# Softmax attention beside linear attention on one core: first loads in use order, a level of sums on GpSimd, a last chain over more banks

## The chip, the cores and the metric

The program runs on one core of a Trainium2 chip. The metric is device time in microseconds. The kernel before took 773.87 us (median of 7 runs, 771.07 to 775.39). A separate profiled execution took 772.23 us; its recorded span is 770.5 us.

## The reference

Two attention layers run on their own inputs, and their outputs are set side by side. In both, S = 2048 tokens, D = 512, H = 32 heads of Dh = 16, and everything is bfloat16.

```python
# A: softmax attention
scores = einsum("bhqd,bhkd->bhqk", q, k) * Dh ** -0.5
o = einsum("bhqk,bhkd->bhqd", softmax(scores), v)
# B: linear attention with a learned feature map
pq, pk = q @ w_phi, k @ w_phi                       # per head, 16 x 16
phi = concatenate([softmax(p), softmax(-p)])        # 32 features, for q and for k
kv, z = einsum("bhsf,bhsd->bhfd", phi_k, v), phi_k.sum(s)
o = (phi_q @ kv) / (phi_q @ z + 1e-6)
# both: o @ wo; out[:, 0:512] is A, out[:, 512:1024] is B
```

## The kernel before

**A.** The work is cut into 32 units: 8 groups g of four heads by 4 chunks c of 512 queries. A unit has 16 key tiles (`kt`, 128 keys). Each key tile of a unit has four pieces, one a head: TensorE multiplies 32 rows of `KT` with 32 rows of `QT` into a bank of PSUM (`kq`, L748). From there a key tile goes one of two ways. On the ScalarE way (`act_kt`, `act_exp`, L962), one activation takes exp of two or three pieces at once. On the VectorE way (`dve_kt`), four `tensor_scalar` (L1020) write the bits of a float16 exponential as uint16, and three more (L1031) shift these by a quarter step each. TensorE then adds V times the exponentials into the unit's bank (L755): four matmuls a key tile for ScalarE, sixteen for VectorE. `src_a` and `src_d` deal the key tiles out as the engines come free, so more room on VectorE means fewer key tiles for ScalarE, and the other way round.

When a unit is complete, VectorE copies its bank to `X` (L803). The sums in it go by DMA to `sums`, VectorE takes reciprocals (L817), two more DMAs spread these to `Yd` (L820, L823), GpSimd multiplies (L835), and every eight units the output projection follows (L1076, L1091, L1094).

**B** runs in between. Its weights are folded with `w_phi` into `Wf`. Sixteen `k_step` make the keys' features for 128 tokens each: two exponentials on ScalarE (L1172), the sum of each 16 on VectorE (L1175), a reciprocal (L1178), two products on GpSimd (L1182), V's projection, and the product with V (L1202, L1211). Sixteen `q_step` do the queries.

**Head.** SP and ScalarE issue the first loads (L575 to L590). Four blocks of 128 rows of x are transposed on TensorE in two halves (L607), each of which ScalarE (L618) or VectorE (L621) copies out; then come the first Q and K projections (`proj`, `first_k`, L649, L693). The weight `va` says up to which key tile ScalarE copies every second V tile out, and `ka` how many of the eight copies of the first pair's K are ScalarE's (L677, L699). For the later K tiles, VectorE copies out (L659), GpSimd masks one copy (L685) and VectorE masks the other in place (L687, stream `dv_ek`).

**Tail.** The last unit doesn't use the DMAs: a matmul with `sel` spreads its sums (L852), VectorE (L862) and ScalarE (L866, L868) take reciprocals, VectorE multiplies (L870), then sixteen matmuls (L877) and four (L883) make the last 512 rows of A, copied out at L1088 and L1091 and stored at L1094. `range_check` (L900) counts sums that are out of range; its flag decides whether `_general`, another whole path, runs. The program ends with a wait for every DMA queue's semaphore.

**Order.** Nothing is decided on the chip. `_Sched` (L158) runs when the program is built: it holds a queue of tasks for each purpose (`SC.stream`), each with a weight, and always places the task with the least start time plus weight, by its own durations and latencies. The outcome is one fixed instruction order per engine, with semaphores between. `_W` holds the weights, and `_AT` changes them after every 16 key tiles. `port=True` marks VectorE work that the planner keeps from lying beside GpSimd's, and each GpSimd task waits for the last such VectorE task (L322). Fill matmuls (L782) keep TensorE at work.

Of the kernel before, what the change touches and what calls it, by code (L numbers as in the profile page):

```python
# [26 lines left out]
class _Stream:  # L27
    def __init__(self, key, sem, step):
        self.key = key
        self.sem = sem  # L30
        self.step = step
        self.seq = 0
        self.items = []
        self.known = {}

# [18 lines left out]
class _Plan:  # L54

    def __init__(self):
        self.streams = {}

# [15 lines left out]
    def dma(self, queue_key, dma_key, fn, deps=()):  # L74
# [3 lines left out]
        d.seq += 1  # L78
        clock = dict(q.known)
# [78 lines left out]
class _Sched:  # L158
# [147 lines left out]
    def _place(self, t, start):  # L306
# [41 lines left out]
        if t.then is not None:  # L348
# [5 lines left out]
          dek=-0.081, av=-0.051, kf=-0.03, v=0.039, kv=0.004, qf=-0.012, y=-0.203, t=0.061, o=0.243, df=-0.163,  # L354
          dred=-0.076, dv=-0.053, dkv=-0.118, dy=-0.02, dd=0.003, dob=-0.078, dmn=0.041, akf=-0.019,
          aqf=-0.089, aot=-0.317, age=0.03, early=0.0, guard=0.346, cut=5, lead=6, b0=0.286, b1=0.54, b2=0.99,
          p0=8, p1=30, p2=6.012, el=2, va=16, ka=8, dm=0.4, force=0.41, fill=0.575, dg=9.0)
_AT = (
    (16, dict(qd_r=0.028, pa_n=4, pd_w=-0.018, dx=-0.13, dev=-0.185, kf=0.191, t=0.016, dred=-0.015, dv=-0.112,
         dkv=-0.099, lead=5, el=3)),  # L360
    (32, dict(dev=-0.176, dad=0.08, av=-0.024, v=-0.015, dred=-0.03, dkv=-0.263, aot=-0.267, cut=6)),
    (48, dict(dx=-0.161, dn=-0.142, da=-0.093, dek=-0.193, o=0.174, dred=0.092, dkv=-0.169)),
    (64, dict(pa_w=0.186, da=-0.041, t=-0.143, dmn=0.088, aqf=-0.05, force=0.401)),
    (80, dict(qa=-0.09, b=-0.016, dek=-0.392, kf=0.176, o=0.066, dy=-0.045, dd=0.081, guard=0.393, force=0.423,
         fill=0.523)),
    (96, dict(qa=-0.035, qd_r=0.115, pa_n=3, pa_w=0.053, pd_w=0.071, b=-0.067, dx=-0.205, dev=-0.361, dn=-0.232,
         da=-0.165, dad=0.033, dek=-0.081, av=-0.051, kf=-0.03, v=-0.004, qf=0.039, t=0.061, o=0.243, dred=-0.076,
         dv=-0.053, dkv=-0.118, dy=-0.02, dd=0.003, dmn=0.089, aqf=-0.113, aot=-0.317, guard=0.346, cut=5, el=2,
         force=0.41, fill=0.575)),
    (112, dict(b=0.054, dv=-0.088, cut=6)),  # L370
    (128, dict(qa=-0.01, qd_o=0.258, pj=-0.023, pa_n=4, dev=-0.337, kf=-0.125, kv=0.138)),
    (144, dict(tp=-0.289, dad=0.017, dek=-0.071, t=0.114, dred=0.027, dy=-0.048, lead=6)),
    (160, dict(df=-0.044, dv=-0.151)),
    (176, dict(pa_n=5, b=-0.012, dev=-0.315, dop=-0.47, dn=-0.205, dek=0.033, t=0.113, df=0.024, dv=-0.086,
         guard=0.24)),
    (192, dict(op=-0.055, o=0.219, dv=-0.15, dd=-0.02)),
    (208, dict(kv=0.114, dv=-0.241, akf=-0.029, force=0.418, dg=1.5)),
    (224, dict(qa=-0.012, qd_r=0.032, pa_n=3, pa_w=-0.038, pd_w=0.067, dxe=-0.184, dop=-0.475, dad=-0.077,
         dek=0.117, av=0.012, v=-0.084, dkv=-0.112, dd=0.046, dob=0.031, aqf=-0.094)),
    (240, dict(b=-0.066, dx=-0.217, dop=-0.41, av=-0.009, v=-0.137, o=0.178, dred=0.076, guard=0.364, fill=0.583)),  # L380
    (256, dict(pd_n=1, op=-0.011, dek=0.165, t=0.142, o=0.381, aqf=-0.185)),
    (272, dict(qd_o=0.274, b=-0.197, dev=-0.216, av=-0.01, t=0.14, dv=-0.326, cut=5, lead=5, force=0.436)),
    (288, dict(pj=-0.091, kf=-0.045, dred=0.192, dy=-0.179, force=0.414)),
    (304, dict(qd_r=0.056, pa_n=2, op=0.004, dev=-0.175, dek=0.12, t=0.103, dd=0.078, el=3)),
    (320, dict(dn=-0.079)),
    (336, dict(qd_r=0.128, b=-0.244)),
# [21 lines left out]
def _main_path(nc, es, P, dsem, flag, A_x, A_wqkv, A_wo, B_x, B_wqkv, B_w_phi, B_wo, out):  # L408
# [440 lines left out]
    def last_unit(xv, xi, c):  # L849
# [6 lines left out]
        for k in range(4):  # L856
            cs = slice(128 * k, 128 * k + 128)
            bc = bcs[k // 2]
            def y_at(t, cs=cs):
                return Yd[:, parts[0][0].res["y"].idx if parts else t.res["y"].idx, cs]  # L860
# [1468 lines left out]
```

## Time and profile before

| what | us |
|---|---|
| median of 7 runs | 773.87 |
| profiled execution, its time | 772.23 |
| its span | 770.5 |
| ScalarE busy | 745.1 |
| TensorE busy | 730.1 |
| VectorE busy | 724.3 |
| GpSimd busy | 151.2 |
| first L962 starts | 10.65 |
| last X copy (L803) starts | 758.05 |

Busy time counts overlapping ends of neighbouring instructions, and TensorE's most of all, since matmuls are pipelined: VectorE's L1020 has a mean of 683 ns, but four in a row took 2.47 us. A line of the stretches view gives a stretch, its length, each engine's busy time with its number of instructions, TensorE's granted clock, and the DMA share and rate. A line of the groups gives the line, engine, operation and tiles, the count, the busy time and the mean, and the idle time before them with what ended it.

### The profile page before, as it was taken

Reading aid. Unit: us, or ns where it says so; the run is one execution under the profiler, and the core shown is the slowest. Engines: PE = TensorE matmul, PEld = TensorE weight load, DVE = VectorE, ACT = ScalarE, POOL = GpSimd, SP = SyncE. Lnnn points to the kernel's source line nnn. Section 1 sums busy time; section 2 is a strip of 40 time slices with the busy share of each in tenths; the row PEclk is TensorE's granted clock in tenths of the full one; section 3 lists DMA queues with packets and bytes.
Section 4 is the critical chain, followed back from the end, with each engine's and each line's share of the span. In section 5 each row is a group of like instructions: output and inputs, shape, how many; then the busy total and the mean of one; then the engine's idle time right before and its main releaser. Section 6 shows DMA issues by size and latency. Waiting matters only on the chain.

```text
span 770.5 us, 17249 instructions
## 1 busy us (share of the span) xinstructions
PE 730.1 (95%) x7209; PEld 217.4 (28%) x7209; DVE 724.3 (94%) x1315; ACT 745.1 (97%) x846; POOL 151.2 (20%) x218
## 2 busy tenths in 40 slices
PE   8999999999899999999999999999999999999996
PEld 3322222223222222223222223322222222222222
DVE  1799999999799999999999999999999999999996
ACT  6999999999799999999999999999999999999994
POOL 3321111110102131312122113232222113122120
PEclk9999999999899999999999999999999999999999
DMA  6200000017300110000000010000000001010002
GB/s 151 69 3 23 11 15 19 16 26 139 97 12 15 30 34 15 6 16 17 18 16 19 16 32 17 9 18 23 26 23 22 26 21 34 16 32 29 11 25 65
DMA packets 43871, 23.38 MB, mean 30 GB/s; under 512 B 31180, under 2 KB 39820, under 8 KB 43788
## 3 DMA queue, kind: packets, MB, share of 16 engines
q1 hardware_dynamic: 42204, 21.45, 10.3%
q8 instruction: 57, 0.93, 0.5%
q10 hardware_dynamic: 1584, 0.79, 0.5%
q14 instruction: 26, 0.21, 0.1%
HBM read 11.81 MB, written 4.45 MB: 21 GB/s over the span
## 4 chain that ended last, share of the span: by engine, by line
ACT 87%; PE 7%; DVE 3%; DMA 2%; issue 0%; SPq 0%; ACTq 0%
ACT pT L962 82%; PE PS L755 2%; PE PS L748 2%; ACT e_k L1172 2%; ACT eT L1235 1%; DMA sums<-X 1%; DVE rg L1020 1%; DMA OT<-in_A_x_dram 1%; DVE rg L1031 1%; ACT Wf L1235 1%; PE PS L877 0%; ACT KT L677 0%; ACT VP L657 0%; DVE Wf L1157 0%; PE PS L646 0%; DMA scr<-rin 0%
## 5 line engine op out<-in xcount | busy, mean ns | idle before, releaser
L962 ACT ACTIVATE pT<-PS 128x1024 bf16<-128x1024 f32 (+1 forms) x755 | 707.0, 1095 | 6.7 <-PE PS L748 6.6
L1020 DVE TENSOR_SCALAR rg<-PS 128x512 uint16<-128x512 f32 x524 | 340.1, 683 | 11.4 <-PE PS L748 9.6
L748 PE MATMUL PS<-QT,KT 32*128 32x512 bf16 x2048 | 318.0, 387 | 21.4 <-ACT pT L962 14.6
L1031 DVE TENSOR_SCALAR rg<-rg 128x2048 uint16<-128x2048 uint16 x393 | 256.5, 688 | 1.3 <-PE PS L755 0.9
L748 PEld LDWEIGHTS PS<-QT,KT 32*128 32x128 bf16 x2048 | 80.6, 91 | 286.5 <-ACT pT L962 226.8
L755 PE MATMUL PS<-pT,VP 128*32 128x512 bf16 x1524 | 151.0, 390 | 4.2 <-ACT pT L962 2.0
L755 PE MATMUL PS<-rg,VJ 128*32 128x512 f16 x1572 | 144.8, 388 | 3.8 <-DVE rg L1031 3.3
L755 PEld LDWEIGHTS PS<-pT,VP 128*32 128x32 bf16 x1524 | 39.1, 94 | 82.5 <-issue 51.3
L1182 POOL TENSOR_TENSOR w<-e_k,stat 128x512 bf16<-128x512 bf16 x32 | 33.1, 1056 | 119.7 <-DVE stat L1178 68.2
L755 PEld LDWEIGHTS PS<-rg,VJ 128*32 128x32 bf16 x1572 | 38.3, 95 | 54.2 <-issue 22.1
L755 PE MATMUL PS<-rg,VP 128*32 128x512 f16 x524 | 52.0, 387 | 0.1
L1282 POOL TENSOR_TENSOR w<-w,den 128x256 bf16<-128x256 f32 x32 | 19.3, 619 | 112.8 <-DVE den L1278 78.9
L835 POOL TENSOR_TENSOR OT<-X,Yd 128x256 bf16<-128x256 f32 x30 | 22.2, 757 | 95.9 <-DMA Yd<-scr 50.1
L835 POOL TENSOR_TENSOR Oo<-X,Yd 128x256 bf16<-128x256 f32 x30 | 22.2, 759 | 83.8 <-DMA Yd<-scr 69.9
L649 PE MATMUL PS<-xT,w 128*128 128x512 bf16 x124 | 36.6, 383 | 0.9 <-DVE xT L621 0.9
L1272 POOL TENSOR_TENSOR w<-w 128x272 f32<-128x272 f32 x32 | 23.7, 758 | 61.4 <-DVE rg L1031 43.2
L1258 DVE TENSOR_TENSOR w<-PS,stat 128x408 f32<-128x408 f32 (+1 forms) x48 | 25.3, 527 | 0.2
L803 DVE COPY X<-PS 128x512 f32<-128x512 f32 x32 | 21.9, 685 | 2.7 <-PE PS L755 2.7
L782 PE MATMUL PS<-ones_t,zer 128*32 128x512 bf16 x252 | 24.2, 388 | 0.0
L685 POOL TENSOR_SCALAR KT<-KT,hmask 128x512 bf16<-128x512 bf16 x12 | 8.3, 692 | 67.9 <-DVE KT L659 45.7
L1175 DVE TENSOR_REDUCE stat<-e_k 128x64 f32<-128x1024 bf16 x16 | 19.4, 1213 | 0.7 <-ACT e_k L1172 0.7
L1294 PE MATMUL PS<-woB,e_k 128*128 128x512 bf16 x64 | 19.4, 384 | 0.0
(103 smaller groups left out, 428.1 us busy)
## 6 DMA issues: line engine op xcount, KB each, us to landing
Yd<-scr SPq DMA_DIRECT2D x31, 256.0 KB
out_dram<-e_k SPq DMA_DIRECT2D x16, 128.0 KB, 1.7
out_dram<-OA SPq DMA_DIRECT2D x12, 128.0 KB, 1.7
OT<-Oo SPq DMA_DIRECT2D x60, 16.0 KB, 1.8
w<-in_A_wqkv_dram SPq DMA_DIRECT2D x2, 384.0 KB, 5.4
OT<-in_A_x_dram SPq DMA_DIRECT2D x1, 512.0 KB, 5.2
w<-in_A_wqkv_dram ACTq DMA_DIRECT2D x1, 512.0 KB, 7.0
WOp<-in_A_wo_dram SPq DMA_DIRECT2D x1, 512.0 KB, 6.5
```

Of the source, the lines that this page charges most:

```text
L649: return e.matmul(bank_of(t), w[:, ct, c0:c0 + 128], xT[:, ct, c * 512:(c + 1) * 512], start=(ct == 0), stop=(ct == 3))
L748: return e.matmul(out_ap, KT[32 * r:32 * r + n, g, kt * 128:(kt + 1) * 128], QT[32 * r:32 * r + n, c, g // 2, :], start=True, stop=True, t ...
L755: return e.matmul(PS[32 * r:32 * r + 32, pvb[u].idx, :], lhs(8 * (g // 2) + 2 * r + g % 2), rhs(r), start=t.res["first"], stop=t.res["last ...
L782: P.op("pe", lambda e, r=r: e.matmul(PS[32 * r:32 * r + 32, pvb[u].idx, :], zer[:], ones_t[:].unsqueeze(1).broadcast_to([128, 4, 128]), st ...
L803: xv = _Task("dve", 0.61, one("dve", lambda e, t: e.tensor_copy(X[:, t.res["x"].idx, :], PS[:, pvb[u].idx, :])), [], lat=DL, need=[("x", x ...
L835: ms.append(put(po_n, _Task("pool", 0.7, one("pool", lambda e, t, cs=cs: e.tensor_tensor(OT[:, c % 2, g // 2, cs] if even else Oo[:, ms[0] ...
L962: return e.activation(pT[:, p:p + n, :].rearrange("p a n -> p (a n)"), PS[:, b:b + n, :].rearrange("p a n -> p (a n)"), ACT.Exp, scale=0.25)
L1020: return e.tensor_scalar(rg[:, q0.res["i"].idx, 512 * r:512 * r + 512], PS[:, qk.res["D"].idx, :], ya, yb, ALU.mult, ALU.add)
L1031: ad = put(dv_ad, _Task("dve", 0.59, one("dve", lambda e, t, j=j: e.tensor_scalar(rg[:, t.res["j"].idx, :], rg[:, q0.res["i"].idx, :], flo ...
L1182: ph.append(put(po_phi, _Task("pool", 1.03, one("pool", lambda e, t, a=a: e.tensor_tensor(pk[ph[0].res["k"].idx][:, 512 * a:512 * a + 512] ...
L1258: muls.append(put(dv_y, _Task("dve", 0.485, one("dve", lambda e, t, yv=yv, lo=lo, n=n: e.tensor_tensor(ysv[r0.res["y"].idx][:, 136 * lo:13 ...
L1272: ad = [put(po_y, _Task("pool", 0.73, one("pool", lambda e, t, k=k: e.tensor_tensor(y3(0)[:, 2 * k:2 * k + 2], y3(0)[:, 2 * k:2 * k + 2], ...
```

## The change

- The narrow K and Q loads and the V load move from ScalarE's DMA queue to SP's, behind x and ahead of the twelve transposing loads of the other chunks.
- x's first chunk is transposed in four quarters, each into its own bank, and copied out by VectorE, ScalarE, VectorE, VectorE. The first K (128 keys) and the first Q projection are summed over these quarters as they come (`first_qk`).
- `va` goes from 16 to 8 and `ka` from 8 to 4: VectorE gets four V copies and the odd half of the first K pair from ScalarE.
- The second mask of the later K tiles moves from VectorE to GpSimd.
- In `k_step`, GpSimd adds each 16 in two halves of 8 (float32, two instructions of 128x256, written where the products go later), and VectorE reduces 8 instead of 16.
- The last unit's X is copied in two halves, its spread matmuls go to three banks, its sixteen first matmuls become tasks of their own that may lie ahead of X, and the four copies alternate between ScalarE and VectorE. Two of the range check's counts are put at the end of the unit before.
- The waits at the end are sorted by when their queue last issued.
- The table `_AT` is replaced as a whole, and with it the whole order on each engine. `_W` is as before but for `va`, `ka` and the dropped `dek`.

```diff
-          p0=8, p1=30, p2=6.012, el=2, va=16, ka=8, dm=0.4, force=0.41, fill=0.575, dg=9.0)
+          p0=8, p1=30, p2=6.012, el=2, va=8, ka=4, dm=0.4, force=0.41, fill=0.575, dg=9.0)
...
-    l_k0 = load_w("k", 0, 128, 3.0, "act")
-    l_q0 = load_w("q", 0, 128, 3.0, "act")
-    l_v = load_w("v", 0, 512, 5.0, "act")
+    l_k0 = load_w("k", 0, 128, 3.6)
+    l_q0 = load_w("q", 0, 128, 3.6)
+    l_v = load_w("v", 0, 512, 4.4)
...
-    for h in range(2):
-        tp = put(pe_tp, _Task("pe", 0.5, pe_group(8, lambda e, t, i, h=h: e.transpose(
...
+    for ct in range(4):
+        tp = put(pe_tp, _Task("pe", 0.26, pe_group(4, lambda e, t, st, ct=ct: e.transpose(
+            PS[:, t.res["b"].idx, :].bitcast(BF)[:, st * 128:(st + 1) * 128], xn[:, st, ct * 128:(ct + 1) * 128], ident[:, :])),
+            [l_x0], lat=PL, need=[("b", A_bank if ct < 2 else G, 1, 1)], pre=[t_ident], area=0.0))
...
+        if ct == 1:
+            x_ev.append(put(ac_xe, _Task("act", 0.49, one("act", lambda e, t, ct=ct, src=src: e.activation(
...
+            x_ev.append(put(dv_xe, _Task("dve", 0.34, one("dve", lambda e, t, ct=ct, src=src: e.tensor_copy(
...
-            k_ready[(2 * a + 1, c)] = put(dv_ek, _Task("dve", 0.27, one("dve", lambda e, t: e.tensor_scalar(
-                odd, odd, hmask[:, 1:2], None, ALU.mult)), [k1], lat=DL, pre=[t_hm], port=True))
+            k_ready[(2 * a + 1, c)] = put(po_k, _Task("pool", 0.65, one("pool", lambda e, t: e.tensor_scalar(
+                odd, odd, hmask[:, 1:2], 0.0, ALU.mult, ALU.add)), [k1], lat=GL, pre=[t_hm]))
...
+    def first_qk():
+        qk = []
+        for ct in range(4):
+            def mm(e, t, i, ct=ct):
+                if i == 0:
+                    return e.matmul(PS[:, qk[0].res["k"].idx, 0:128], w[:, ct, 512:640], xT[:, ct, 0:128],
+                                    start=(ct == 0), stop=(ct == 3))
+                return e.matmul(PS[:, qk[0].res["b"].idx, :], w[:, ct, 0:128], xT[:, ct, 0:512], start=(ct == 0), stop=(ct == 3))
+            qk.append(put(pe_tp, _Task("pe", 0.28, pe_group(2, mm), [x_ev[ct], l_k0, l_q0], lat=PL,
+                                       need=[] if ct else [("b", G, 1, 1), ("k", G, 1, 2)])))
...
+            xvs.append(_Task("dve", 0.34 if last else 0.61, one("dve", lambda e, t, k=k: e.tensor_copy(
+                X[:, xvs[0].res["x"].idx, n * k:n * k + n], PS[:, pvb[u].idx, n * k:n * k + n])),
...
             if u == NU - 2:
+                n = 16 * (NU - 1)
+                early = count(sums[:, 0:n], _A_LO, ALU.is_ge, 0, col[:], 0.66)
+                checked.append(count(sums[:, 0:n], _SUM_HI, ALU.is_le, 1, [early], 0.66))
...
+        bcs = [put(pe_ls, _Task("pe", 0.45, spread(2, lambda i: slice(128 * i, 128 * i + 128), lambda i: i), [xvs[0]], lat=PL,
+                                pre=[t_sel], need=[("b", A_bank, 1, 2), ("y", y_sl, 1, 4), ("o", oo_sl, 1, 1)])),
+               put(pe_ls, _Task("pe", 0.45, spread(1, lambda i: slice(256, 512), lambda i: 0), [xvs[1]], lat=PL,
+                                need=[("b", A_bank, 1, 1)]))]
...
+        r0 = put(dv_l, _Task("dve", 0.95, one("dve", lambda e, t: e.reciprocal(
...
+        r1 = on_act(128, 128, bcs[0])
+        r23 = on_act(256, 256, bcs[1])
...
+                [f, ms[st]] + fours[-1:], lat=PL))
+            out_rows(c, st, f, t, n)
...
+    def last_firsts(c):
+        for st in (1, 0, 2, 3):
+            for p in range(4):
+                fours.append(put(pe_op, _Task("pe", MM, pe_group(1, lambda e, t, i, p=p, st=st: e.matmul(
+                    bank_of(firsts[st]), OT[:, c % 2, p, st * 128:(st + 1) * 128], WOp[:, p, :] if p < 3 else WOl[:, 0, :],
+                    start=(p == 0), stop=False)), [mul[8 * c + (1, 3, 5, 6)[p]], l_wo] + wol,
+                    need=[] if p else [("b", G, 1, 1)], gate=lambda: state["ua"] >= NU and not pend and not pe_qd["q"])))
+                firsts.setdefault(st, fours[-1])
...
-            rd = put(dv_red, _Task("dve", 1.13, one("dve", lambda e, t: e.tensor_reduce(
-                stat[:, t.res["s"].idx, 0:64], e_k[:, f.res["e"].idx, :].rearrange("p (g f) -> p g f", f=16),
-                AX.X, ALU.add)), exps, lat=DL, need=[("s", st_sl, 1, 3)]))
+            hs = []
+            for a in range(2):
+                hs.append(put(po_r, _Task("pool", 0.7, one("pool", lambda e, t, a=a: e.tensor_tensor(
+                    half(hs[0].res["k"])[:, 32 * a:32 * a + 32], ek8(f.res["e"], a)[:, :, 0:8], ek8(f.res["e"], a)[:, :, 8:16],
+                    ALU.add)), [exps[a]] + folds, lat=GL, need=[] if a else [("k", pk_sl, 1, 1)])))
+            rd = put(dv_red, _Task("dve", 0.62, one("dve", lambda e, t: e.tensor_reduce(
+                stat[:, t.res["s"].idx, 0:64], half(hs[0].res["k"]), AX.X, ALU.add)), hs, lat=DL, need=[("s", st_sl, 1, 3)]))
...
-        if last and st < 3:
+        if last is not None and last % 2 == 0:
...
-        ends = [k for k, t in P0.streams.items() if t.step == 16 and t.seq > 0]
+        ends = sorted((k for k, t in P0.streams.items() if t.step == 16 and t.seq > 0), key=lambda k: P0.streams[k].last)
```

## The prediction

> **What bounds it now.** I read the page's busy shares and chain first, since they say which engine's work is worth removing.
>
> ```profile
> span 770.5 us, 17249 instructions
> PE 730.1 (95%) x7209; PEld 217.4 (28%) x7209; DVE 724.3 (94%) x1315; ACT 745.1 (97%) x846; POOL 151.2 (20%) x218
> ACT 87%; PE 7%; DVE 3%; DMA 2%; issue 0%; SPq 0%; ACTq 0%
> ```
>
> ScalarE (ACT) is the chain for 87% of the span, and VectorE (DVE) is nearly as full. GpSimd (POOL) has four fifths of its time free. Second, the view by stretches, to see where ScalarE is not full.
>
> ```profile
> 0.00:10.00 10.00, 7.16 (x40) 3.33 (x41) 2.46 (x4) 2.76 (x4) 4.17 (x15) 1.00 0.83 198
> 10.00:20.00 10.00, 10.00 (x56) 3.35 (x55) 2.04 (x3) 9.97 (x15) 1.93 (x3) 1.00 0.54 106
> 20.00:30.00 10.00, 9.68 (x75) 3.26 (x74) 7.26 (x13) 9.97 (x14) 5.20 (x8) 1.00 0.36 117
> 30.00:40.00 10.00, 10.00 (x78) 3.23 (x77) 7.26 (x12) 8.92 (x12) 2.98 (x5) 1.00 0.01 2
> 184.00:206.00 22.00, 19.34 (x187) 5.93 (x184) 18.41 (x32) 17.64 (x18) 1.29 (x2) 0.84 0.73 156
> 245.00:275.00 30.00, 27.91 (x273) 8.00 (x270) 27.56 (x49) 27.80 (x31) 4.53 (x6) 0.94 0.09 29
> ```
>
> ScalarE (fourth busy figure) loses time at the head, at the tail, 4.4 us at 184 to 206 and 2.2 us at 245 to 275. VectorE (third) has 13.4 us free between 10 and 40, while ScalarE is full there and TensorE nearly so. Third, the groups, for prices.
>
> ```profile
> L962 ACT ACTIVATE pT<-PS 128x1024 bf16<-128x1024 f32 (+1 forms) x755 | 707.0, 1095 | 6.7 <-PE PS L748 6.6
> L1020 DVE TENSOR_SCALAR rg<-PS 128x512 uint16<-128x512 f32 x524 | 340.1, 683 | 11.4 <-PE PS L748 9.6
> L1031 DVE TENSOR_SCALAR rg<-rg 128x2048 uint16<-128x2048 uint16 x393 | 256.5, 688 | 1.3 <-PE PS L755 0.9
> L1175 DVE TENSOR_REDUCE stat<-e_k 128x64 f32<-128x1024 bf16 x16 | 19.4, 1213 | 0.7 <-ACT e_k L1172 0.7
> L1282 POOL TENSOR_TENSOR w<-w,den 128x256 bf16<-128x256 f32 x32 | 19.3, 619 | 112.8 <-DVE den L1278 78.9
> L687 DVE TENSOR_SCALAR KT<-KT,hmask 128x512 bf16<-128x512 bf16 x12 | 4.2, 352 | 0.5 <-POOL KT L685 0.5
> ```
>
> **The exchange rate.** 524 first steps at four a key tile are 131 key tiles on VectorE; the other 381 are ScalarE's. A key tile costs ScalarE 707.0 / 381 = 1.86 us and VectorE (340.1 + 256.5) / 131 = 4.55 us. Both are full and key tiles can be dealt to either, so work taken from one is shared. If X us leave ScalarE and n key tiles come back to it, the end moves by T = X - 1.86 n = 4.55 n, which is T = 0.71 X. If Y us leave VectorE, T = Y - 4.55 n = 1.86 n, which is 0.29 Y.
>
> **Head.** These timeline rows carry it (start, duration):
>
> ```profile
> 0.91 0.46 SPq L581 DMA_DIRECT2D OT<-in_A_x_dram  x1
> 1.12 4.27 PE L601 MATMUL PS<-ones_t 128*128 128x512 bf16 x12 [1.12 <-POOL ones_t L447]
> 6.24 1.05 PE L607 MATMUL PS<-ident,OT 128*128 128x128 bf16 x16 [0.85 <-DMA OT<-in_A_x_dram]
> 10.65 1.02 ACT L962 ACTIVATE pT<-PS 128x1024 bf16<-128x1024 f32 x1
> ```
>
> x lands at 6.1, 5.2 us after its issue. The DMA rates by 0.75 us of the first 6 us add up to 0.92 MB, and x is 0.52 MB of it; had x gone first, that sum passes 0.52 MB by 3.75 us. The warm-up matmuls hold TensorE until 5.4, so the transposes gain at most 0.85 us. The Trainium skill (DMA: Bandwidth & Descriptors, Issuing engines are not separate DMA queues) says that a second issuing engine saves only issue time, while its transfers interleave. By the rule alone the move costs the three issues that ScalarE did beside (1.58 us in all) on SP; the row says that the interleaving held x back for longer than that. K and Q then land behind x, near 6.5.
>
> From transposes to Q's copy the old path is 1.05 for sixteen transposes with 1.0 of copying, then 1.26 of matmuls. In quarters: first quarter 0.45 with latency; VectorE's three copies, 0.42 each by the row of 128x512 bfloat16 (L1291), end 1.8 after the start; the last pair of matmuls 0.3; Q's copy 0.69; the first QK and its way to ScalarE 0.7, as now. From 5.4 that is 8.9, and 0.3 more if K and Q are a little late: first exp near 9.2 in place of 10.65: **-1.4** (bounds 0, if K and Q land at 8, and -2.0). SP's twelve transposes start 1.6 us later for the three loads ahead of them, as do the wide K, Q and output weight loads behind these: chunk 1 lands near 12.3, where its K projection ran at 15.5; chunk 2 near 17.7 against 23.5; chunk 3 near 23 against 32.7. V is fourth in the queue, near 8, and its first projection ran at 10.35. All are covered; without cover each costs up to 1.6.
>
> **Copies from ScalarE to VectorE.** ScalarE loses four V copies at 0.61, three K copies at 0.70 and the 128- and 384-wide pair, 0.9 (two of L699's four, 1.8 in all): 5.5 us. VectorE gains about as much between 12 and 40, inside its 13.4 free us, so nothing; without that cover it would be 5.5 x 0.29 = 1.6. At the rate above ScalarE's loss is worth 3.9. But TensorE is packed there too, and the chain of the head runs over its V projections between 26 and 33. Bounds 0 and -3.9; I take **-2.5**.
>
> **VectorE to GpSimd.** L1175 has 1024 elements at 1213 ns; at one element per 1.04 ns (VectorE at 0.96 GHz, VectorE: DVE Perf Modes, Specifications, of the Trainium skill) its fixed part is 146 ns, and 512 float32 elements take 680: 16 x 0.53 = 8.5 us. The twelve masks L687 are 4.2. Two counts of the range check, 1.3 us, come in from the tail. Net 11.4, times 0.29: **-3.3**.
>
> GpSimd takes 32 additions, 128x256. The near rows are 619 ns (L1282) and 727 (L835, same size); I take 0.70, 22 us, and 12 x 0.69 = 8 us for the masks. GpSimd has room: a `k_step` lasts about 12 us (from 229 to 419 for sixteen) and would hold 3.5 us of it.
>
> One rule speaks against this. SBUF — State Buffer (SBUF: two separate sides) says that GpSimd and VectorE's two-port operations exclude each other for a whole instruction. L1031 is such work, a third of VectorE's time. By the rule alone up to 30 us of new GpSimd work could stand in VectorE's way. The rows: L1031 has a median of 687 ns and a mean of 688, so all its meetings with 218 GpSimd instructions cost some 0.4 us; L835 has a mean of 758 against a median of 727. The planner keeps such work apart, so I go by the row: 0.1 us.
>
> The new coupling costs more: VectorE's reduction now waits for GpSimd, which itself waits for the last planned L1031. Behind the waiting reduction stand L1020 and L1031 of all key tiles, for whose banks and results TensorE waits, and then ScalarE. The plan puts the reduction where the sums should be ready. Bounds 0 and 16 x 1.4 (both additions exposed) = 22; taken by the nearest wait of that kind, VectorE's L687 behind GpSimd's L685, 0.5 us in twelve, for 32 additions: **+1.3**. The longer K mask chain on GpSimd has key tiles of slack.
>
> **Tail.**
>
> ```profile
> 758.05 0.69 DVE L803 COPY X<-PS 128x512 f32<-128x512 f32 x1 [0.41 <-PE PS L755]
> 758.80 1.13 PE L852 MATMUL PS<-X,sel 128*128 128x256 f32 x4 [0.26 <-DVE X L803]
> 763.64 1.58 ACT L1088 ACTIVATE rg<-PS 128x512 bf16<-128x512 f32 x3 [1.62 <-PE PS L883]
> 764.26 1.81 SPq L1094 DMA_DIRECT2D out_dram<-rg  x4
> ```
>
> X leads to the spread, then to 3.45 us of the sixteen matmuls (L877, 0.216 each), four more, the copies, and four stores 0.45 apart. The reciprocals are done earlier (761.2 to 763.2 with their products) and lose the range check's 1.3 us between them, so they stay off the path. The gain is what of the 3.45 us lies ahead of X. They need the product of unit 31 (L828, done 757.64), and banks, of which X's and B's last ones hold some: all behind the spread would give -0.4, and twelve ahead -2.2. I take about seven ahead, 1.5. The end waits in a new order leave out some seven waits behind the last store's landing, perhaps 0.3. **-1.8** (bounds -0.4, -2.5).
>
> **Sum.** -1.4 - 2.5 - 3.3 + 0.1 + 1.3 - 1.8 = -7.6: 764.6 for the profiled execution of 772.2. That is 1.6 below the median of the runs, so for the median **766.3**.
>
> The whole order is redrawn, which I can't cost. Its lost time now is the two stretches above (6.6 us of ScalarE) and 1.3 elsewhere. The larger comes from SP's queue: the loads of B hold it from 171 to 194, a unit's sums are sent at 193.9 and take 4.4 us, and VectorE waits 2.6 us. Nothing changed removes that. I take it as equal, within 4 us either way.
>
> **The rivals.**
>
> *The body doesn't gain* (0.20). TensorE is bound where ScalarE is relieved, and the moved key tiles' twelve extra matmuls fill it. For it: 95% busy, and 10.00 of 10 at the head. Against it: its busy time overlaps, and it has time for 252 fill matmuls. Head and tail alone, less half: about 771.5, with 769.5 to 773.
>
> *The stalls go too* (0.12). The new order places the unit's reciprocal behind the sums' landing and the clock stays full: a further -4 and more, 762. For it: 7.9 us lost in all; against it: the same queue.
>
> *VectorE waits for GpSimd* (0.15), the case that ends slower. Place: the reduction in each `k_step`, 230 to 430. GpSimd's additions wait for an L1031 or stand behind a unit's pair of L835 (1.45 us), and VectorE's fixed order can't pass the reduction. At 1.2 us a step, sixteen steps cost 19, of which exponentials already under way may hide a third. Without the 1.3 above, the rest gains 8.9: 773.9 - 8.9 + 13 = 778. It decides from 8.9 / 16 = 0.56 us a step. Against it: sums have a whole step's length to be ready in.
>
> **How the numbers follow.** The likeliest case, 0.53, has 762.5 to 769.5 for its own range. With the rivals' ends, leaving out the far parts of the first and last, the range is 760.5 to 774.5. About 0.2%, or 1.55 us, is what can be told from no change. Faster: all of the likeliest and of the stalls' case, and 0.13 of the body's rival: 0.78. Same: 0.07 of the body's rival. Slower: 0.15.
>
> **What would show it.** The first L962 starts near 9.2; the reduction takes 0.68 us and GpSimd's additions 0.70, and GpSimd's busy time rises by 30 us to about 181; VectorE's key tiles rise from 131 to about 134 (two to four more L1020 groups), and L962's pieces fall by as many; VectorE's idle time before the reduction stays under 2 us; L1031's mean stays at 0.69. X's copy starts near 752, and the last store is issued about 6.5 us after it, where it is now 8.0 (764.26 + 1.81 - 758.05). A stall before the reduction of over 0.5 us a step, or ScalarE's idle time between first and last exp well over 8 us, would make the forecast wrong.

## The result

The changed kernel takes 768.68 us (median of 26 runs, 765.40 to 776.94) against 773.20 (63 runs, 770.96 to 775.39): ratio 0.9942, 95% interval 0.9933 to 0.9952, or 4.5 us faster. The forecast was 766.3, 7.6 us faster. The profiled execution took 768.49 us with a span of 766.8.

The page of the kernel after, its first lines and the shares of the chain:

```profile
span 766.8 us, 17285 instructions
PE 730.4 (95%) x7203; PEld 217.1 (28%) x7203; DVE 724.9 (95%) x1308; ACT 743.2 (97%) x841; POOL 181.7 (24%) x262
ACT 71%; DVE 14%; PE 13%; issue 1%; DMA 1%; POOL 0%; POOLq 0%
```

ScalarE, VectorE and TensorE are as full as before; VectorE and TensorE now hold 27% of the chain where they had 10%. GpSimd's busy time rose by 30.5 us. The view by stretches (columns as before):

```profile
0.00:10.00 10.00, 8.88 (x46) 4.24 (x46) 3.20 (x7) 2.61 (x4) 4.17 (x15) 1.00 0.80 184
10.00:20.00 10.00, 9.75 (x60) 3.08 (x59) 3.89 (x6) 9.71 (x14) 1.93 (x3) 1.00 0.52 102
20.00:30.00 10.00, 9.83 (x74) 3.02 (x74) 7.76 (x14) 8.97 (x12) 3.30 (x5) 1.00 0.51 135
30.00:40.00 10.00, 9.98 (x67) 3.31 (x65) 7.64 (x13) 7.84 (x10) 3.87 (x6) 1.00 0.01 2
184.00:206.00 22.00, 21.27 (x228) 6.94 (x228) 22.00 (x38) 22.00 (x25) 1.00 (x1) 1.00 0.82 169
206.00:245.00 39.00, 36.01 (x361) 10.20 (x357) 35.94 (x62) 36.60 (x42) 10.01 (x12) 0.96 0.08 25
718.00:731.00 13.00, 11.57 (x101) 3.55 (x98) 10.38 (x22) 10.69 (x12) 7.27 (x12) 0.87 0.15 47
```

The stall at 184 to 206 is gone (ScalarE 22.00 of 22, full clock). In its place ScalarE loses 2.4 us at 206 to 245 and 2.3 at 718 to 731. Between 10 and 40, where the change took work from ScalarE, its busy time fell from 28.85 to 26.51: part of what was taken off became idle time. The groups:

```profile
L995 ACT ACTIVATE pT<-PS 128x1024 bf16<-128x1024 f32 x760 | 712.0, 1125 | 7.0 <-PE PS L763 6.2
L1053 DVE TENSOR_SCALAR rg<-PS 128x512 uint16<-128x512 f32 x520 | 335.7, 684 | 9.7 <-PE PS L763 8.5
L1064 DVE TENSOR_SCALAR rg<-rg 128x2048 uint16<-128x2048 uint16 x390 | 260.9, 710 | 0.4
L1219 DVE TENSOR_REDUCE stat<-w 128x64 f32<-128x512 f32 x16 | 10.8, 676 | 0.1
L1216 POOL TENSOR_TENSOR w<-e_k 128x256 f32<-128x256 bf16 x32 | 20.9, 669 | 81.4 <-DVE rg L1064 24.8
L861 POOL TENSOR_TENSOR OT<-X,Yd 128x256 bf16<-128x256 f32 x30 | 23.1, 789 | 139.4 <-DMA Yd<-scr 125.6
```

L995, L1053, L1064 and L861 are the old L962, L1020, L1031 and L835. Three rows matter. The reduction takes 676 ns, was 1213, and waits 0.1 us in all. VectorE has 520 first steps, 130 key tiles, one fewer than before in place of three more, so ScalarE has one more (five pieces more in the first row). And L1064's mean rose from 688 to 710 ns.

From the start of the first exponential to the end of the last, both profiled executions need 746.9 us (10.65 to 757.54 before, 10.40 to 757.30 after). Nearly the whole difference of this pair lies behind X's first copy, from which to the end of the span it was 12.44 us and is 8.83:

```profile
757.94 0.76 DVE L823 COPY X<-PS 128x256 f32<-128x256 f32 x2 [2.03 <-PE PS L770]
758.48 1.09 PE L879 MATMUL PS<-X,sel 128*128 128x128 f32 x6
760.26 0.38 PE L916 MATMUL PS<-WOl,OT 128*128 128x512 bf16 x1
760.48 1.03 PE L905 MATMUL PS<-WOl,Oo 128*128 128x512 bf16 x4
761.52 1.79 SPq L1127 DMA_DIRECT2D out_dram<-rg  x4
763.36 0.45 SPq L1344 DMA_DIRECT2D out_dram<-e_k  x1
764.25 0.15 DVE L941 TENSOR_SCALAR flag<-PS 1x1 int32<-1x1 f32 x1 [0.26 <-PE PS L939]
```

A's last store is issued 5.4 us after X's copy starts (8.0 before), and the program ends 3.5 us after that (4.4).

**The clock as a ruler.** Each execution has its mean granted TensorE clock. A straight line through the changed kernel's 28 recorded executions (0.981 to 0.999) falls by 6.0 us per 0.01 of clock; through 73 of the kernel before (0.986 to 0.997), by 4.1. Read at 0.993 the lines give 768.6 and 772.0. Medians of few runs differ by their clocks too, so the table has both, the last column by each kernel's own line. The clock is in part a kernel's own doing (it falls after TensorE has run thin, last section), so this column also takes out some of what an order does.

| kernel | median us | ratio (95%) | at 0.993 |
|---|---|---|---|
| changed | 768.7 | 0.9942 (0.9933-0.9952) | 768.6 |
| before + tail only | 773.4 | 1.0009 (0.9992-1.0027) | 772.4 |
| changed, 8 warm-ups | 766.8 | 0.9934 (0.9912-0.9957) | 767.3 |
| changed, narrow additions | 767.2 | 0.9945 (0.9923-0.9967) | 767.5 |
| changed, narrow products | 764.0 | 0.9892 (0.9872-0.9912) | 765.0 |
| changed, tail of before | 766.0 | 0.9937 (0.9914-0.9959) | 769.0 |
| changed, waits unsorted | 765.1 | 0.9923 (0.9897-0.9949) | 766.3 |
| changed, table of before | 789.3 | 1.0229 (1.0192-1.0267) | - |
| before, table of after | 790.5 | 1.0250 (1.0225-1.0275) | - |
| changed, head copies twice | 771.8 | 0.9978 (0.9961-0.9995) | 771.5 |
| changed, exps twice | 774.9 | 1.0031 (1.0010-1.0052) | 774.8 |
| changed, reductions twice | 774.6 | 1.0022 (1.0000-1.0043) | 773.1 |
| before, narrow products | 770.5 | 0.9969 (0.9954-0.9984) | 769.9 |

The kernel before itself reads 771.3 to 772.9 at 0.993 in the four sets of runs, and the changed kernel with unsorted waits, whose trace shows no difference in cost, 2.3 less than the changed kernel. So a difference of 2 us between two rows of this column decides nothing; the two with exchanged tables ran at clocks too far off for it.

### The profile page after: what moved, and what is told of

The parts are those of the page before. It is cut to its first block, busy times and chain, and to the rows that moved or that the text cites. A ratio compares the mean times of both kernels' runs of the same rounds, so it can differ in the third digit from the quotient of the medians.

```text
span 766.8 us, 17285 instructions
## 1 busy us (share of the span) xinstructions
PE 730.4 (95%) x7203; PEld 217.1 (28%) x7203; DVE 724.9 (95%) x1308; ACT 743.2 (97%) x841; POOL 181.7 (24%) x262
## 4 chain that ended last, share of the span: by engine, by line
ACT 71%; DVE 14%; PE 13%; issue 1%; DMA 1%; POOL 0%; POOLq 0%
ACT pT L995 68%; DVE rg L1053 6%; DVE rg L1064 5%; PE PS L763 4%; PE PS L770 3%; ACT e_k L1211 2%; ACT eT L1278 2%; PE PS L650 1%; PE PS L653 1%; PE PS L607 1%; DMA sums<-X 1%; DVE Wf L1190 1%; PE PS L1337 0%; PE PS L916 0%; DVE X L823 0%
## 5 line engine op out<-in xcount | busy, mean ns | idle before, releaser
L995 ACT ACTIVATE pT<-PS 128x1024 bf16<-128x1024 f32 x760 | 712.0, 1125 | 7.0 <-PE PS L763 6.2
L1053 DVE TENSOR_SCALAR rg<-PS 128x512 uint16<-128x512 f32 x520 | 335.7, 684 | 9.7 <-PE PS L763 8.5
L1064 DVE TENSOR_SCALAR rg<-rg 128x2048 uint16<-128x2048 uint16 x390 | 260.9, 710 | 0.4
L861 POOL TENSOR_TENSOR OT<-X,Yd 128x256 bf16<-128x256 f32 x30 | 23.1, 789 | 139.4 <-DMA Yd<-scr 125.6
L1325 POOL TENSOR_TENSOR w<-w,den 128x256 bf16<-128x256 f32 x32 | 20.1, 648 | 96.1 <-PE PS L1331 53.3
L1216 POOL TENSOR_TENSOR w<-e_k 128x256 f32<-128x256 bf16 x32 | 20.9, 669 | 81.4 <-DVE rg L1064 24.8
L861 POOL TENSOR_TENSOR Oo<-X,Yd 128x256 bf16<-128x256 f32 x30 | 21.7, 741 | 76.8 <-DMA Yd<-scr 38.3
L823 DVE COPY X<-PS 128x512 f32<-128x512 f32 (+1 forms) x33 | 22.1, 671 | 3.8 <-PE PS L770 3.7
L1211 ACT ACTIVATE e_k<-PS 128x512 bf16<-128x512 f32 x32 | 19.6, 741 | 0.0
```

The lines of the kernel that those rows point to most:

```text
L861: ms.append(put(po_n, _Task("pool", 0.7, one("pool", lambda e, t, cs=cs: e.tensor_tensor(OT[:, c % 2, g // 2, cs] if even else Oo[:, ms[0] ...
L995: return e.activation(pT[:, p:p + n, :].rearrange("p a n -> p (a n)"), PS[:, b:b + n, :].rearrange("p a n -> p (a n)"), ACT.Exp, scale=0.25)
L1053: return e.tensor_scalar(rg[:, q0.res["i"].idx, 512 * r:512 * r + 512], PS[:, qk.res["D"].idx, :], ya, yb, ALU.mult, ALU.add)
L1064: ad = put(dv_ad, _Task("dve", 0.59, one("dve", lambda e, t, j=j: e.tensor_scalar(rg[:, t.res["j"].idx, :], rg[:, q0.res["i"].idx, :], flo ...
L1211: exps = [put(ac_kf, _Task("act", 0.49, one("act", lambda e, t, a=a: e.activation(e_k[:, f.res["e"].idx, 512 * a:512 * a + 512], bank_of(f ...
```

## The experiments

The theory after the first traces: head and tail gained, and the body gained nothing because VectorE's time that was freed went to meetings with GpSimd. The rivals: the tail's edits don't do it either; the freed time is not worth what the sum says; the redrawn order takes it.

### The tail alone

```diff
 # before.py with the change's last_unit, last_firsts, range_check, sorted waits; head, k_step and _AT as before
+        bcs = [put(pe_ls, _Task("pe", 0.45, spread(2, ...
+    def last_firsts(c):
+        ends = sorted(...)
```

> The kernel before with the tail's part of the change alone (X in two halves, the spread over three banks, the sixteen first matmuls as tasks of their own, the counts of the range check ahead of the last unit, alternating copies, sorted waits at the end). The order on every engine is that of the kernel before up to the last unit, so nothing else moves. Theory 1 (nearly all of the change's gain is its tail, 3.6 us by the two profiles, 12.45 to 8.86 from the X copy to the span's end): 3 to 4 us faster than before, a ratio of 0.995 to 0.996. Rival (the tail is worth the 1.8 us of the prediction and the rest of the 4.5 us comes from head and body): 1.5 to 2.2 us faster, 0.997 to 0.998.

No gain. TensorE's and VectorE's rows at the end:

```profile
759.86 0.76 DVE L814 COPY X<-PS 128x256 f32<-128x256 f32 x2 [0.74 <-PE PS L761]
763.64 0.68 DVE L844 TENSOR_TENSOR OT<-X,Yd 128x512 bf16<-128x512 f32 x1
764.38 0.39 PE L907 MATMUL PS<-WOl,OT 128*128 128x512 bf16 x1 [2.29 <-DVE OT L844]
767.20 1.03 PE L896 MATMUL PS<-WOl,Oo 128*128 128x512 bf16 x4
```

L844 is the product of unit 30. In this order its reciprocal stands at 755.83 (748.82 before, 742.40 in the changed kernel), and its product behind the X chain. The sixteen first matmuls are one queue, so they wait for it: TensorE is idle for 2.29 us, and A's last store comes 10.2 us after X, in place of 5.4. The chain over more banks gains nothing in an order that finishes unit 30 so late.

### The tail undone, and the end waits undone

```diff
 # changed kernel without the hunks of the tail; up to unit 30 the order is the same
-        for x in x_all[u]: ...
+        put(dv_x, xev[u])
```

> The changed kernel with its loads, head, GpSimd work and table, but with the tail of before: one copy of X, one bank for the spread sums, the sixteen matmuls and both counts where they were. The sorted waits stay. Up to the end of unit 30 the order of the work is that of the changed kernel. The prediction's term (tail -1.8, of which 0.3 are the waits that stay): 1.5 us slower than the changed kernel, ratio 0.996 to before. The rival, from the two traces (start of X's copy to the end of the span 12.45 before, 8.86 after): about 3 us slower than the changed kernel, ratio 0.998, so that nearly the whole gain is the tail's. If it is 0.994 again, the tail's own edits gave nothing and the body did.

```diff
-        ends = sorted((k for k, t in P0.streams.items() if t.step == 16 and t.seq > 0), key=lambda k: P0.streams[k].last)
+        ends = [k for k, t in P0.streams.items() if t.step == 16 and t.seq > 0]
```

> The changed kernel with the waits at the end of the program in their old order; nothing else moves. The prediction's term 0.3: ratio 0.9946 to before. By the two traces (last issue to the end of the span 4.43 before, 2.99 after) up to 1.4 us slower: ratio 0.996. No change at all (0.994) if the flag's chain is last in either order.

By ratio the two can't be told from the changed kernel, and for the first of them such a result (0.9937) was named in advance as the sign that the tail's own edits give nothing. The traces say more, from X's first copy on:

| kernel | X to A's last store | to the span's end |
|---|---|---|
| before | 8.02 | 12.44 |
| before, narrow products | 8.02 | 12.59 |
| before + tail only | 10.17 | 12.58 |
| changed, tail of before | 8.02 | 10.42 |
| changed, waits unsorted | 5.37 | 8.82 |
| changed | 5.37 | 8.83 |

With the tail of before the end comes 1.6 us later. What the change puts ahead of X instead, eleven of the sixteen matmuls and the two counts, costs next to nothing there: from the 600th exponential to the end of the last, the changed kernel with 8 warm-ups takes 155.5 us and the one with the tail of before 155.4, both with one step at half clock. So by the traces the chain is worth about 1.5, as forecast. By whole times it isn't shown: at 0.993 of clock the tail of before is 2.7 us slower than the kernel with unsorted waits and 0.4 slower than the changed kernel. The other 2.0 us of the 3.6 are a wait at the end, in the last line of this view of SP's waits in the kernel before:

```profile
SPq L1094 <- ACT rg L1088: 4.4, 1, 4.4
...
SPq L2235 <- DMA out_dram<-rg: 2.0, 1, 2.0
```

The same wait is 2.2 us in the kernel before with narrow products. It is missing from the two kernels whose sorted waits follow four such stores (the tail alone, and the changed kernel with the tail of before): there SP goes through its fourteen waits without a stop, 0.06 us each. In the changed tail the order of the waits is worth nothing, since the flag (ready at 764.40, then 0.48 to load it) comes later than the stores. The wait is for the last of A's stores. It landed 4.0 and 4.1 us after its issue in the two traces that wait (765.62 to 769.60, and 762.40 to 766.52), and 1.8 us after in the two that don't. Why it was late, and whether the order of the waits has to do with it, no run shows, so it stays open whether these 2.0 us are the change's own.

### The warm-ups

```diff
-    for i in range(12):
+    for i in range(8):
```

> The changed kernel with 8 warm-up matmuls in place of 12; no other instruction differs. Theory 1 (the head gained 0.25 us where 1.4 was forecast because the twelve warm-up matmuls, at half clock until 6.4, hold the transposes although x has landed by 5.1): transposes start at 5.1 to 5.3, the first exponential at 9.4 to 9.8 in place of 10.4, and 0.5 to 1 us of that reaches the end. Rival (the head after that is bound by the V projections on TensorE, so an earlier first exponential is given back by idle time of ScalarE before 40): the first exponential comes earlier and the time stays within 0.3 us.

Its ratio is that of the changed kernel, and its trace doesn't decide: the clock rose to full speed 3.8 us into the span, early enough for twelve too. What sets the head is the moment of that rise. The changed kernel's profiled execution and the one with narrow additions, both with twelve warm-ups:

```profile
1.12 5.30 PE L607 MATMUL PS<-ones_t 128*128 128x512 bf16 x12 [1.12 <-POOL ones_t L452]
6.21 1.51 PE L613 MATMUL PS<-ident,OT 128*128 128x128 bf16 x16
10.40 1.02 ACT L995 ACTIVATE pT<-PS 128x1024 bf16<-128x1024 f32 x1 [0.17 <-PE PS L763]
```

```profile
1.12 4.24 PE L607 MATMUL PS<-ones_t 128*128 128x512 bf16 x12 [1.12 <-POOL ones_t L452]
5.19 1.06 PE L613 MATMUL PS<-ident,OT 128*128 128x128 bf16 x16
8.92 1.02 ACT L995 ACTIVATE pT<-PS 128x1024 bf16<-128x1024 f32 x1 [0.17 <-PE PS L763]
```

In the first the clock rose at 7.2, in the second at 4.1. Over ten traces with the new head the rise lies between 3.8 and 7.2 and the first exponential between 8.92 and 10.40, in the same order but for 0.1 us; their mean is 9.4. In the old head, where x's landing sets the start, it is 10.46 to 10.65 for rises at 4.2, 5.0 and 6.1 (and 10.23, with x landed 0.4 us sooner, in the one trace of it under the new table). So the head's gain is 1.1 us in the mean, and the profiled pair happened to show 0.25.

### The additions and the products on GpSimd

```diff
 # e3: half of the keys' sums left out
-                    half(hs[0].res["k"])[:, 32 * a:32 * a + 32], ek8(f.res["e"], a)[:, :, 0:8], ek8(f.res["e"], a)[:, :, 8:16],
+                    half(hs[0].res["k"])[:, 32 * a:32 * a + 1], ek8(f.res["e"], a)[:, 0:1, 0:8], ek8(f.res["e"], a)[:, 0:1, 8:16],
 # e4: 31 of 32 of A's normalised values left out
-                    OT[:, c % 2, g // 2, cs] if even else Oo[:, ms[0].res["o"].idx, cs], X[:, xi, cs],
+                    OT[:, c % 2, g // 2, cs.start:cs.start + 8] if even else Oo[..., cs.start:cs.start + 8], ...
```

> The changed kernel with GpSimd's new additions cut from 128x256 to 128x8; VectorE's reduction takes 8 of each 16 exponentials straight, still 512 elements, so B's key features lack half of their sums. The order is the same on every engine. Theory 1 (port: VectorE's L1064 was lengthened by meeting GpSimd's reads, 9.1 us in 27 meetings against 2.1 in 8 before, of which the additions' own six meetings are 1.4 us): L1064's mean falls from 710 ns to 704 to 707, the time by 0.5 to 1.5 us. Rival A (VectorE waits for the additions, the coupling of the prediction): the waits before the reduction vanish and the time falls by 2 us or more. Rival B (neither): within 0.3 us.

> The changed kernel with GpSimd's two products at each unit's end cut from 128x256 to 128x8 (31 of 32 columns of A's normalised values are left out); two memsets are added on GpSimd in the head, where it is idle. The order is otherwise the same. Theory 1 (port: the products' twelve meetings with L1064, 4.6 us, are the largest part of what took VectorE's gain): L1064's mean falls from 710 ns to 695 to 700, and the time falls by 1.5 to 4 us. Rival (buffers hide these stretches, since ScalarE is the chain): L1064's mean falls and the time stays within 0.5 us.

Narrow additions change nothing that can be measured: neither their length nor the reduction's wait for them costs time. Narrow products save 3.9 us (0.0050 of 773, give or take 1.7). Their meetings with L1064, the first candidate, look so, VectorE's and GpSimd's rows of the changed kernel:

```profile
122.29 1.21 DVE L1064 TENSOR_SCALAR rg<-rg 128x2048 uint16<-128x2048 uint16 x1
123.42 0.68 DVE L1053 TENSOR_SCALAR rg<-PS 128x512 uint16<-128x512 f32 x1
...
121.53 1.41 POOL L861 TENSOR_TENSOR Oo<-X,Yd 128x256 bf16<-128x256 f32 x2 [14.22 <-DMA Yd<-scr]
```

The two products end at 122.94, 0.65 us after L1064's start, and L1064 takes 0.52 us longer than its 0.69. It is the same in the others: an L1064 that starts beside a GpSimd instruction ends about 0.55 after that one's end. Counting every L1064 over 0.75 us, with its excess over 0.69, by the GpSimd instruction that it overlaps:

| trace | L1064 so stretched | VectorE's time in it | of it by the products |
|---|---|---|---|
| before | 8 of 393 | 2.1 us | 1.6 |
| changed | 27 of 390 | 9.1 | 4.6 |
| changed, narrow additions | 17 | 6.4 | 2.7 |
| changed, narrow products | 12 | 3.0 | 0 |
| changed, tail of before | 22 | 6.2 | 1.5 |
| changed, waits unsorted | 23 | 8.0 | 3.4 |

In the changed kernel the rest is the products of `k_step` 1.5, the additions 1.4, B's last products 1.4, the masks 0.2. The planner prices a unit's product at 0.70, and the trace has 0.74 to 0.79, two in a row: the L1064 that it puts right behind comes too early.

But most of the saving lies elsewhere. The runs that keep the changed kernel's table and list of tasks have its order (the one with the tail of before up to unit 30), so their 760 exponentials (L995) can be matched one by one. From the first to the last, the run with narrow products is 3.8 us shorter than the changed kernel, and 2.7 of this lie in one stretch, 719 to 740 us, where GpSimd and TensorE of the changed kernel show:

```profile
723.50 1.41 POOL L861 TENSOR_TENSOR Oo<-X,Yd 128x256 bf16<-128x256 f32 x2 [2.94 <-DMA Yd<-scr]
724.87 1.65 POOL L1325 TENSOR_TENSOR w<-w,den 128x256 bf16<-128x256 f32 x2
726.65 0.28 PE L1288 MATMUL PS<-KVbd,eT 128*128 128x144 bf16 x2 [1.41 <-POOL w L1325]
731.15 0.69 DVE L1053 TENSOR_SCALAR rg<-PS 128x512 uint16<-128x512 f32 x1 [2.11 <-PE PS L763]
```

The unit's two products wait for their DMA and stand ahead of a product of `q_step` (L1325) on GpSimd. TensorE, whose order is fixed too, waits for that one, the clock falls to half at 727.4, and VectorE and ScalarE run dry. TensorE waits there for 1.1 to 2.0 us in all eight traces of this order with whole products, and these twenty exponentials take 19.4 to 22.6 us. With narrow products it doesn't wait, and they take 18.4.

Leave out this stretch and the one from 206 to 226 us, where a late DMA makes it 16.7 to 19.5 us in traces of the same instructions. Then the narrow products are 0.8 to 1.7 us ahead of four runs (changed, 8 warm-ups, tail of before, unsorted waits), while their L1064 are stretched by 3.2 to 6.1 us less. So a stretched L1064 costs 0.2 to 0.3 of its stretch, and the theory that the meetings took the body's gain falls: the 7.0 us that the change added would be 1.4 to 2.1.

The same cut in the kernel before:

> The kernel before in its own order, with GpSimd's products of a unit at 8 of their 256 columns (31 of 32 of A's normalised values are left out), as in the run on the changed kernel that came out at 0.9892, some 0.5% below the changed kernel itself. If what that run saved is the meetings that are new with the change (VectorE's long integer step stretched by 2.1 us in all in the trace of before, of it 1.6 by the products, against 7 to 9 us after): under 1 us here, ratio 0.999 to 1. If the products cost some 3 us in any order, by holding GpSimd or by being late: ratio near 0.996.

It saves 2.4 us there (give or take 1.2), with 1.55 us less stretching, and the two savings differ by less than their errors. Its trace doesn't explain it: 2.8 of 3.2 us lie between 188 and 207 us, where VectorE waits for the DMA of a unit's sums. That wait is 2.6 us before, 1.9 here, and 4.3 in the run with the tail alone, which has the old order there too; elsewhere 0.3 us is saved.

### The tables exchanged

```diff
 # e7: all edits, _AT of before.   e8: before.py, _AT of the changed kernel
-    (16, dict(dev=-0.308, dv=-0.102)),
+    (16, dict(qd_r=0.028, pa_n=4, pd_w=-0.018, dx=-0.13, dev=-0.185, kf=0.191, ...
```

> All edits of the change, but planned with the table of before. If the edits carry the gain, as the prediction's sum has it, the table is worth little: within 2 us of the changed kernel, ratio 0.994 to 0.997. If the redrawn order carries it, the edits under a table that was not drawn for them lose more in stalls of ScalarE than they save: slower than before, ratio 1.003 or above, with ScalarE idle well over 9 us between its first and last exponential.

> The kernel before, planned with the changed kernel's table, no edit of the code. If the new table is simply a better one, faster than before: ratio 0.997 or below. If a table is only good for the code that it was drawn for: slower than before, ratio 1.003 or above, by idle time of ScalarE in the body.

Both are 2.3 to 2.5% slower than before. Between first and last exponential ScalarE is idle 17.0 and 13.8 us in their traces, against 8.9 in the changed kernel and 7.8 before. The kernel before with the new table, 200 to 240 us:

```profile
200.00:240.00 40.00, 34.17 (x282) 8.32 (x284) 30.94 (x51) 29.23 (x32) 5.89 (x7) 0.79 0.24 66
```

ScalarE loses 10.8 of 40 us and the clock is 0.79. A table is good for one list of tasks alone: an order not fitted to the code costs some 18 us, four times what the whole change gains. This also rules out taking single edits of the body back under either table.

### Work done twice in the fixed order

To price an engine's time without a new order, three runs leave the order as it is and do an instruction twice, the first time into a tile not used yet.

```diff
+    # e9: the copies of K and V that ScalarE still does in the head; e10: one of two exponentials of each k_step
+    P.op("act", lambda e: e.activation(eT[:, 0, 0, :], <same source>, <same function>))
+    # e11: each reduction of k_step
+    P.op("dve", lambda e: e.tensor_reduce(eT[:, 0, 0, 0:128].bitcast(F32), half(...), AX.X, ALU.add))
```

> The changed kernel in its own order, with the eight copies of K and V that are still on ScalarE in the head (about 10 to 45 us; four of V, three of K at 512 and one at 384) each done twice, the first time into a tile that is not used yet: some 4.5 us more of ScalarE there. By the prediction's rate (0.71 of ScalarE's time, by which it gave the copies taken from ScalarE 2.5 us): 3.2 us slower than the changed kernel, ratio near 0.998 to before. If ScalarE's time in the head is worth nothing because TensorE is the bound there (ScalarE idle 3.5 us between 10 and 40 us, TensorE busy 9.75 to 9.98 of 10): under 1 us, ratio 0.993 to 0.995.

> The changed kernel in its own order, with one of the two exponentials of B's k features on ScalarE done twice in each of the 16 steps (the first time into a tile that is not used yet): some 9.6 us more of ScalarE in the stretch of those steps. By the rate 0.71: 6.8 us slower than the changed kernel, ratio near 1.003 to before. If ScalarE sets the pace alone there: 9.6 us, ratio 1.007. If TensorE or VectorE does: under 2 us, ratio below 0.997.

> The changed kernel in its own order, with each of the 16 reductions of B's k sums on VectorE done twice (0.676 us each, 10.8 us more of VectorE, near to the 8.5 us that the change took from it in the same place). By the prediction's rate (0.29 of VectorE's time): 3.1 us slower than the changed kernel, ratio near 0.998 to before. If the time that the change saved on VectorE is worth nothing in this order: under 1 us, ratio 0.993 to 0.995. If VectorE sets the pace there: up to 10.8 us, ratio 1.008.

The added groups in the three traces:

```profile
L666 ACT ACTIVATE eT<-PS 128x512 bf16<-128x512 f32 x4 | 2.6, 647 | 0.0
L687 ACT ACTIVATE eT<-PS,hmask 128x512 bf16<-128x512 f32 x3 | 2.1, 688 | 1.7 <-PE PS L657 1.7
L717 ACT ACTIVATE eT<-PS,hmask 128x384 bf16<-128x384 f32 x1 | 0.6, 580 | 0.2 <-PE PS L727 0.2
```

```profile
L1216 ACT ACTIVATE eT<-PS 128x512 bf16<-128x512 f32 x16 | 12.2, 762 | 0.0
```

```profile
L1224 DVE TENSOR_REDUCE eT<-w 128x64 f32<-128x512 f32 x16 | 10.8, 673 | 0.0
```

Counted from start to start, so without the overlapping ends, these are 4.1, 7.7 and 9.5 us (the expectations had 4.5, 9.6 and 10.8). Against the changed kernel's ratio they cost 2.8, 6.9 and 6.2 us, each give or take 1.5 to 1.8: 0.7, 0.9 and 0.65 of the time added. Exponentials matched as above, outside the two stretches, give 3.5, 6.4 and 5.9. The theory that ScalarE's time in the head is worth nothing falls. For VectorE 0.65 is twice the prediction's 0.29. The two are different prices: 0.29 is worked out for time that the planner knows of and shares out as key tiles; here the order is fixed, nothing is shared out, and only slack makes it cheaper than 1. Nor is 0.65 the price of all VectorE time: that of the stretched L1064 is 0.2 to 0.3.

## Why the prediction was right, and where it wasn't

The time lay within the range and on the forecast's side, 3.1 us short of the gain. That it came so near is in part luck: the body, which was to bring 4.4 us, brought nothing that can be measured, and the tail brought twice its 1.8, by a wait that nobody had counted. By its steps:

- **Head, -1.4.** Right in mechanism; 1.1 in the mean of ten traces. x lands 4.2 us after its issue in place of 5.2. (The working had it at 3.75 us into the span; the DMA rates of the kernel before, added up, pass 0.52 MB only by 4.5. With the warm-ups until 5.4 that changed nothing.) The step took the warm-ups' end at 5.4 as fixed, but that end moves with the clock's rise, which the old head hid behind x's landing. V and the transposed chunks behind x in the queue cost nothing that shows.
- **Copies from ScalarE to VectorE, -2.5.** Half of it shows. ScalarE's copies take 4.5 us less, its idle time between 10 and 40 us grew by 2.3, and it ran three pieces more there (30 for 27 between 9 and 45). But VectorE's copies did not lie in free time: they added 5.4 us and its busy time in that stretch rose by 2.7 (16.57 to 19.29): between 9 and 45 it did 14 first steps (L1053) for 16 and 8 of L1064 for 9. That ScalarE's time there is worth about 0.7 was run only in the opposite direction.
- **VectorE to GpSimd, -3.3.** The prices were right: 676 ns for 680, 669 for 700, the masks' 3.1 to 4.2 us gone. The step that failed is the exchange, "work taken from one is shared". VectorE was dealt 130 key tiles, where 134 were forecast, and ScalarE 382, one more than before. So between the first and the last exponential ScalarE had 738.0 us of work after 739.1: its copies of K and V took 4.0 less, its exponentials of the scores 2.9 more. The deal is made when the program is built, so nothing that only the chip adds can be the reason. Why the new plan deals so, no run shows.
- **The port rule, +0.1.** Mis-sized. L1031's mean less its median hid what meetings cost: counted one by one, that trace has eight stretched L1031, by 2.1 us and not 0.4. And they were few because the planner had kept them apart there, which was read as a property of the instructions ("so I go by the row"). The Trainium skill's page SBUF — State Buffer (SBUF: two separate sides), cited against it, was right in kind: an L1064 that starts beside a GpSimd instruction waits for that one's end. In size it lies between the two: 7.0 us more of VectorE's time, where the row was read as 0.4 and the rule allowed 30. At 0.2 to 0.3 this comes to some 1.4 to 2.1 us, worked out and not run by itself.
- **Coupling, +1.3.** Nearly nothing: 0.1 us of waiting before the reduction, and narrow additions bring nothing. The rival that VectorE waits for GpSimd in `k_step` is false. TensorE does wait for GpSimd, at another place, in `q_step` at 725.
- **Tail, -1.8.** The chain's 1.5 holds (1.6), given an order that finishes unit 30 early, but not by its own sum: eleven matmuls lie ahead of the spread, not seven, and A's last store comes 2.65 us sooner after X, of which the flag's chain, now last, lets 1.6 through. The prediction named that unit's product (as "unit 31", counted from one), but took its place in the order as given. The waits' 0.3 were 2.0 by the traces, for a store that landed late.
- **"I take it as equal"**, the redrawn order. Both old stalls moved rather than stayed, and ScalarE's idle time went from 7.8 to 8.9 us, 2.4 of it behind the unit's product at 723. That is near equal; that an order can cost 18 us when it isn't fitted shows how much rests on this line.

Taken by parts, the gain of 4.5 is about 1.1 at the head and 3.6 at the tail, so the body, which was to bring 4.4, brought nothing within the 1.5 us or so that these terms leave. (Of the tail's 3.6, 2.0 are the store that landed late in both traces of the old end. Were it on time in other executions of the kernel before, the body's part would be larger by as much.) VectorE's account from 10 to 757 us, start to start: 11.6 us freed by reduction and masks, and 4.6 by 4 first steps and 3 L1064 fewer (one key tile). Against these stand 7.4 in longer L1064, 5.4 in copies of K and V, 1.9 in the reciprocals of the queries' sums (L1298, not longer at 278 ns for 284, but less covered by their successors), 1.3 in the counts. This is the rival "the body doesn't gain" in its result; its reason, TensorE full where ScalarE is relieved, covers at most the head. Shown are that no key tiles came over and what the stall at 719 to 740 costs; what the new order gave or took otherwise in the body stays open: no run has the edits and a second order fitted to them.

## What to carry to other kernels

A rate at which freed time is shared out among engines holds only if the plan shares it out: count the pieces that each engine was dealt, before the time. Before work goes to GpSimd, price the meetings on a shared port that a new order will make, not those that the old one avoided, and look who stands behind whom in its fixed order: here one product ahead of another cost as much as all the new meetings. Two executions of one order can be compared instruction by instruction, which shows where a difference lies when medians can't. And an edit at the end of a program is worth what the order around it allows: look for the last input of each queue there, not only for the chain.

## What was not expected of the hardware

The clock falls to half in whole steps of 3.4 us: in the changed kernel at 212 and at 727 us, once each, in the kernel before for 6.8 us at 198.7 and for 3.4 at 270.4. These are the places where TensorE has just run thin (the stretches with 0.84, 0.94, 0.96 and 0.87 in the tables), so a stall there costs itself and then a step or two at half clock. In ten executions of the changed kernel's variants the first rise to full clock lay anywhere from 3.8 to 7.2 us into the span, also a range of 3.4. One execution, that with unsorted waits, had no step at all between its head and its last matmuls, a mean clock of 0.999, and the shortest span of all, 760.7 us. A SyncE wait on a semaphore that is already up took 0.06 us at the end of the program, and a flag's load 0.48.
